# Heads of q and k crossed between the slots of a tile at the load, v loaded as it lies

## The chip, the cores and the metric

The kernel runs on one core of a Trainium2 chip, in one launch. The time is the device time of one execution in microseconds; the median of several executions is compared. The core has five engines with an instruction stream each: TensorE (PE in the profile, its weight loads PEld), VectorE (DVE), ScalarE (ACT), GpSimd (POOL) and SyncE (SP), which here issues DMAs. Sixteen DMA engines move the data. An engine takes its instructions strictly in the order of its stream and waits where one's input is not there yet.

## The reference

Eight batches, eight heads, 576 tokens, 64 numbers per head. First a Nystrom attention with 32 landmarks, each the mean of 18 neighbouring tokens; then a normalization and a two-layer network over the 512 features of all heads, added to the attention's output.

```python
q_lm = q.reshape(B, H, 32, 18, D).mean(axis=3)        # k_lm likewise
A  = softmax(scale * q    @ k_lm.T)                   # 576 x 32
Bm = softmax(scale * q_lm @ k_lm.T)                   # 32 x 32
C  = softmax(scale * q_lm @ k.T)                      # 32 x 576
Z  = Bm.T / (norm_1(Bm) * norm_inf(Bm) + 1e-6)
for _ in range(6): Z = 2 * Z - Z @ Bm @ Z
y  = A @ Z @ C @ v                                    # per head; heads side by side: x
xn = (x - mean(x)) / sqrt(var(x) + 1e-6) * g_ln
out = x + maximum(xn @ w_ch1, 0) @ w_ch2              # w_ch1 512 x 2048, w_ch2 2048 x 512
```

## The kernel before

**Units and tiles.** A unit is four heads of one batch, so a batch has two units (`u` = 0 and 1). Each of q, k and v is loaded per unit as one staging tile `stg` of 128 partitions x 2 slots x 9 x 64 numbers (`load`, L309). The four heads are numbered 2r + e: `e` is the half of the partitions (64 partitions each, nine tokens per partition, which are one row of 2304 bytes in DRAM), `r` the slot in the free dimension. A ring of six staging tiles holds what is on its way; a buffer becomes free when its tile has been cast to fp16. q and k are cast into `nat` tiles by GpSimd, a few by ScalarE, and v into `natv` by GpSimd.

**Attention of batches 1 to 7** is done in sets: batch 1, batch 2, batches 3 and 4, batches 5 and 6, batch 7 (`sets`, class `Coming`). VectorE transposes each `nat` tile in 32x32 blocks into `xT`. After that, TensorE works in tiles of 32x32: partition block p_ of xT holds half of the tokens of one head, and a matmul names its row block `rb` and its column block `cb` in the array; `cb` is also the partition block of PSUM that gets the result. `scores_k` (L965) computes the landmark scores of k (psec), `scores_q` those of q (psea), `attention2` (L1014) the landmark-landmark scores (psb), the product with v (pscv), the iteration for Z (st), and then zt and zc. For units of odd number the column blocks of `scores_k` are turned by two, so that two units work in different places of the array. The transposed scores then hold the two halves of the tokens' partitions exchanged, and for the product with v the odd units' v has to be exchanged likewise: `load_swapped` (L316) loads it in two DMAs of 64 partitions each, L320 (288 KB each).

**zt** (L1130 to L1145): for every unit and head, the transposed product of Z and C v, in one pair of PSUM banks (`pszt`), copied to SBUF in one instruction by the engine that is free sooner (`sooner`). `pszc` is the same product the other way round; masked by `heads_of` it becomes `zcbd`, with which `rows_of` computes the attention's output rows. The first layer of the network never forms the normalized input: `First.products` (L1264) multiplies zt with the scaled w1 per head (`m16`), and `chunk` multiplies `m16` with the scores `ea`.

**The network's layers** run on whole 128x128 arrays: `first_layer` in 16 chunks per batch (psh to hT), `second_layer` over hT and w2. From batch 4 on the second layer uses seven half-size products in place of eight (`seven_products`).

**Order.** The load of batch 0, of the weights and of batch 1 stands in a fixed order in the text (L1723 to L1752): w1, then batch 1's k, k, q, q, three pieces of w2, batch 1's two v tiles, the other five pieces of w2; the casts on GpSimd stand in the same order. Everything after comes from `run()`: five streams (attention, totals, first layers, the first rows, second layers) and helpers (loads, casts, transposes, statistics, stores) are interleaved by a planner while the program is written. It keeps a model of every engine and of the DMA (`Clock`, with bytes at 385 per ns) and takes the next step whose time has come. The table `AFTER` overrules it: an entry (a, i): (b, n) holds step i of stream a back until stream b has taken n steps. What comes out is a fixed instruction order on each engine. Stores and loads share SP's stream.

Of the kernel before, what the change touches and what calls it, by code (L numbers as in the profile page):

```python
# [20 lines left out]
def kernel(  # L21
# [293 lines left out]

    def load_swapped(src, b, u, queue):  # L316
        t = stage.tile([P, 2, NJ, D], FP32, name="stg", tag="stg")
        halves = src[b, 4 * u:4 * u + 4].rearrange("(r e) (t j) d -> e t r j d", e=2, j=NJ)
        for e in range(2):
            keep(queue.dma_start(out=t[ts(1 - e, 64), :, :, :], in_=halves[e]))  # L320
        return t
# [48 lines left out]
    for x in range(2):  # L370
        for e in range(2):
            nc.gpsimd.tensor_copy(out=heads4[:, x, :, e], in_=mask4[:, ts(e ^ x, 2)])
    heads_of = [heads4[:, x, :, :].rearrange("p r e -> p (r e)") for x in range(2)]
    spread16 = const.tile([P, 2, 2, 2, LM], FP16, name="spread16")
    nc.gpsimd.memset(spread16[:], 0.0)
# [397 lines left out]
    class Coming:  # L773
# [91 lines left out]
        def load(self, i, queue=nc.sync):  # L865
            nm, w = self.parts[i]
            b, u = self.units[w]
            src = {"q": q, "k": k, "v": v}[nm]
            self.stg[i] = stage.pin(load_swapped(src, b, u, queue) if nm == "v" and u % 2
                                    else load(src, b, u, queue))  # L870

# [93 lines left out]
    def scores_k(pair, lm, xT):  # L965
        tiles = {w: ps2.tile([P, 2, 512], FP32, name="psec", tag="p2") for w in pair}
        for r in range(2):
            for x in range(2):
                for w in pair:
                    for p_ in range(4):  # L970
                        rows = ts(p_, 32)
                        cb = 32 * ((p_ + 2 * (w % 2)) % 4)
                        MM(tiles[w][ds(cb, 32), r, 0:NJ * LM], lm["q", w][rows, r, :, x],
                           xT["k", w][rows, r, :, :, x], rb=32 * p_, cb=cb,
                           start=(x == 0), stop=(x == 1), skip=True)
# [16 lines left out]
    def scores_q(pair, lm, xT):  # L992
        tiles = {w: ps2.tile([P, 2, 512], FP32, name="psea", tag="p2") for w in pair}
        for s_ in range(2):
            for x in range(2):
                for w in pair:
                    for p_ in range(4):
                        e, half = divmod(p_, 2)
                        r = half ^ s_
                        rows = ts(p_, 32)  # L1000
                        cb = 32 * (2 * (e ^ (w % 2)) + r)
                        MM(tiles[w][ds(cb, 32), half, 0:NJ * LM], lm["k", w][rows, r, :, x],
# [11 lines left out]
    def attention2(bs, c):  # L1014
# [10 lines left out]
        for y in range(W // 2):  # L1025
# [5 lines left out]
            for w in pair:  # L1031
                for x in range(2):
                    for p_ in range(4):
                        rows, r = ts(p_, 32), p_ % 2
                        MM(psb[rows, w, :], lm["q", w][rows, r, :, x], lm["k", w][rows, r, :, x],
                           rb=32 * p_, cb=32 * p_, start=(x == 0), stop=(x == 1), skip=True)
            if y == W // 2 - 1:
# [91 lines left out]
        cv, z0 = cv_[0], 2 * (bs[0] % 2) if W == 2 else 0  # L1129
        yield lambda: clock.both(clock.at(st, cv), asm.next("zt"))  # L1130
        pszt = ps2.tile([P, 2, 512], FP32, name="pszt", tag="p2")

        def cv_of(w, p_, at, n):
            return cv[ts(p_, 32), w, ds((D + 1) * (p_ % 2) + at, n)]

        for w in range(W):
            for p_ in range(4):
                e, r = divmod(p_, 2)
                sl = ds(32 * p_, 32)
                for half in range(2):  # L1140
                    cb = 64 * e + 32 * half
                    MM(pszt[ds(cb, 32), r, ds(LM * w, LM)], cv_of(w, p_, 32 * half, 32), st[sl, w, LM:],
                       rb=32 * p_, cb=cb)
        zt = asm.pin(asm.tile([P, 2, W, LM], FP16, name="zt", tag="zt"))
        sooner(2 * W * LM)(zt[:].rearrange("p r w l -> p r (w l)"), pszt[:, :, 0:W * LM])  # L1145
        pszc = ps2.tile([P, 2, 512], FP32, name="pszc", tag="p2")
        for w in range(W):
            for p_ in range(4):
                sl = ds(32 * p_, 32)
                cb = 32 * ((p_ + 2 * (w % 2)) % 4)  # L1150
                MM(pszc[ds(cb, 32), w % 2, ds(D * (w // 2), D)], st[sl, w, LM:], cv_of(w, p_, 0, D),
# [9 lines left out]
        for w in range(W):  # L1161
            dve.tensor_tensor(
                out=zcbd_buf[z0 + w][:],
                in0=pszc[:, w % 2, None, ds(D * (w // 2), D)].broadcast_to([P, 4, D]),
                in1=heads_of[w % 2][:, :, None].broadcast_to([P, 4, D]),
                op=ALU.mult)
# [78 lines left out]
    class First:  # L1245
# [18 lines left out]
        def products(self, f, psm):  # L1264
# [3 lines left out]
            for r in range(2):  # L1268
                for e in range(2):
                    for u, (w, _) in enumerate(self.units):  # L1270
                        rows, cb = ds(64 * e, 64), 32 * (2 * (e ^ u) + r)
                        MM(psm[u][ds(cb, 32), :], self.zt[rows, r, w, :],
# [301 lines left out]
    def help_out(hurry=False):  # L1574
# [68 lines left out]
    AFTER = {  # L1643
        (0, 21): (4, 68), (0, 64): (4, 197), (0, 66): (2, 79), (0, 72): (4, 251),
        (0, 80): (4, 269), (0, 93): (4, 314), (0, 101): (4, 496), (0, 108): (4, 528),
        (0, 116): (2, 149), (2, 25): (0, 3), (2, 28): (4, 16), (2, 66): (4, 129),
        (2, 89): (4, 219), (2, 96): (0, 82), (2, 108): (4, 333), (3, 5): (4, 2), (4, 10): (0, 13),
        (4, 33): (0, 16), (4, 140): (0, 40), (4, 171): (0, 55), (4, 433): (2, 133),
        (5, 19): (0, 31), (5, 24): (2, 53), (9, 8): (4, 238),
    }  # L1650
# [134 lines left out]
```

## Time and profile before

| | |
|---|---|
| median of three runs | 272.34 us (270.92 to 272.78) |
| profiled execution | 272.2 us |
| its span, first to last instruction | 270.5 us |
| TensorE busy | 257.0 us, 95% |
| VectorE, ScalarE, GpSimd busy | 202.9, 174.0, 133.9 us |
| DMA packets of the SP queue | 23288, 46.02 MB, 55.5% of sixteen engines' span |
| DMAs issued | 146 |

The profile is one execution. The row PE of its slices shows TensorE's busy share in 40 slices of 6.76 us, in tenths; the row DMA the mean busy share of the sixteen DMA engines; GB/s what they moved. A completion of a DMA is itself a small packet and is counted with the packets under 512 B. "Idle before" in a timeline, in brackets behind an instruction, is the time for which its engine had nothing to do, and what ended it. Lines L296 and L302 are helpers through which all instructions of the engines pass, so the tiles' names tell the groups apart.

### The profile page before, as it was taken

The page shows a single profiled execution, that of the slowest core. Times are in us where ns is not written, and L with a number is a line of the kernel's source. Part 1 is how long each engine was busy: PE and PEld are TensorE (multiplying, and loading weights), DVE is VectorE, ACT ScalarE, POOL GpSimd, SP SyncE. Part 2 cuts the span into 40 slices and gives each one's busy share as a digit, 9 for nine tenths or more (in the row PEclk, how much of TensorE's full clock was granted, in tenths as well). Part 3 has the DMA queues.
Part 4 walks back from the last instruction along what each step waited for, and adds up shares of the span by engine and source line. Part 5 has one row for each costly group of instructions (what it writes and reads, how often), then busy time and mean ns, then how long its engine had stood idle before and what let it go on. Part 6 is the DMA issues. An engine that isn't in the chain of part 4 may idle for free.

```text
span 270.5 us, 8330 instructions
## 1 busy us (share of the span) xinstructions
PE 257.0 (95%) x3442; PEld 167.7 (62%) x3442; DVE 202.9 (75%) x461; ACT 174.0 (64%) x335; POOL 133.9 (49%) x161
## 2 busy tenths in 40 slices
PE   6789996999999999999999999999999999999992
PEld 6644663456553674546655456687868865788881
DVE  2557772599999996998973896799863699948751
ACT  2578893377856978589987659678488645872000
POOL 5286757999947669979999937100000014000000
PEclk9999998899999999999999999999999999999999
DMA  7999999999998998936900120110060006100616
GB/s 252 379 395 376 344 255 385 367 278 311 334 286 224 323 334 246 279 136 197 233 21 22 46 63 16 41 39 4 2 155 0 4 20 148 35 0 17 141 30 166
DMA packets 23486, 46.68 MB, mean 173 GB/s; under 512 B 2324, under 2 KB 2584, under 8 KB 23448
## 3 DMA queue, kind: packets, MB, share of 16 engines
q1 hardware_dynamic: 23288, 46.02, 55.5%
q8 instruction: 27, 0.44, 0.7%
q10 hardware_dynamic: 160, 0.13, 0.2%
q14 instruction: 11, 0.09, 0.1%
HBM read 36.70 MB, written 9.44 MB: 171 GB/s over the span
## 4 chain that ended last, share of the span: by engine, by line
PE 56%; DVE 18%; DMA 12%; ACT 5%; issue 3%; POOL 2%; SPq 1%; ACTq 0%; POOLq 0%; DVEq 0%
PE bank L302 37%; PE psh L302 14%; DMA stg<-in_v_dram 6%; DMA stg<-in_q_dram 3%; DMA wstg<-in_moe_w_ch_dram 3%; DVE m L296 3%; DVE part L296 3%; DVE xblk L296 2%; DVE xT L296 2%; ACT hT L296 2%; DVE six L296 2%; PE psd L302 1%; ACT xblk L296 1%; PE pscv L302 1%; DVE hT L296 1%
## 5 line engine op out<-in xcount | busy, mean ns | idle before, releaser
L302 PE MATMUL bank<-w,hT 128*128 128x512 f16 (+3 forms) x528 | 111.1, 335 | 2.5 <-POOL w L296 2.5
L296 ACT ACTIVATE hT<-psh 128x576 f16<-128x576 f32 x115 | 71.5, 654 | 19.0 <-PE psh L302 17.9
L302 PEld LDWEIGHTS <-hT 128*128 128x128 f16 x656 | 60.4, 98 | 34.4 <-issue 9.7
L302 PE MATMUL psh<-ea,m 128*128 128x288 f16 x512 | 78.6, 286 | 0.9 <-DVE ea L296 0.5
L302 PEld LDWEIGHTS <-m 128*128 128x128 f16 x512 | 48.9, 97 | 20.4 <-issue 3.9
L296 DVE SCALAR_TENSOR_TENSOR xblk<-bank,rstd,xblk 128x256 f32<-128x256 f32 (+2 forms) x77 | 39.2, 541 | 20.4 <-PE bank L302 17.6
L296 POOL TENSOR_TENSOR ea<-ea,lns 128x576 f16<-128x576 f16 x14 | 18.2, 1309 | 56.0 <-ACT lns L296 53.7
L296 POOL CAST nat<-stg 128x1152 f16<-128x1152 f32 x23 | 26.5, 1164 | 7.9 <-DVE sT L296 5.0
L296 DVE BATCH_NORM_STATS2 six<-xblk 128x6 f32<-128x512 f32 x36 | 24.2, 673 | 2.6 <-ACT xblk L296 2.6
L296 POOL CAST natv<-stg 128x1152 f16<-128x1152 f32 x16 | 18.2, 1163 | 13.2 <-DMA stg<-in_v_dram 10.5
L296 ACT COPY xblk<-bank 128x512 f32<-128x512 f32 (+1 forms) x35 | 20.0, 595 | 4.6 <-PE bank L302 4.2
L296 DVE STREAM_TRANSPOSE xT<-nat 128x576 uint32<-128x576 uint32 x28 | 21.2, 757 | 0.0
L302 PE MATMUL bank<-w2mix 128*128 128x256 f16 x128 | 17.4, 273 | 0.0
L296 ACT ACTIVATE lns<-psd 128x576 f32<-128x576 f32 x16 | 10.3, 646 | 9.4 <-PE psd L302 9.3
L296 DVE SCALAR_TENSOR_TENSOR st<-st,bank 128x128 f16<-128x128 f16 (+2 forms) x36 | 11.0, 307 | 6.5 <-PE bank L302 6.2
L302 PE MATMUL bank<-w2mix,hT 128*128 128x256 f16 x128 | 15.8, 273 | 0.0
L296 ACT ACTIVATE ea<-psea 128x576 f16<-128x576 f32 x14 | 8.4, 650 | 10.3 <-PE psea L302 10.3
L296 ACT CAST m<-bank 128x512 f16<-128x512 f32 x19 | 10.4, 587 | 6.6 <-PE bank L302 6.5
L302 PE MATMUL bank<-zcbd,ea 128*128 128x256 f16 x80 | 14.5, 273 | 0.0
L296 DVE TENSOR_REDUCE part<-xT 128x32 f16<-128x576 f16 x20 | 14.3, 744 | 0.2
L296 DVE SCALAR_TENSOR_TENSOR m<-less,zsum,bank 128x512 f16<-128x512 f16 (+1 forms) x18 | 11.5, 678 | 3.5 <-ACT hT L296 1.4
L302 PEld LDWEIGHTS <-w2mix 128*128 128x128 f16 x128 | 12.4, 98 | 2.1 <-issue 0.2
(135 smaller groups left out, 361.9 us busy)
## 6 DMA issues: line engine op xcount, KB each, us to landing
stg<-in_q_dram SPq DMA_DIRECT2D x16, 576.0 KB, 6.4
stg<-in_k_dram SPq DMA_DIRECT2D x16, 576.0 KB, 6.7
out_dram<-xblk SPq DMA_DIRECT2D x70, 128.0 KB, 2.4
wstg<-in_moe_w_ch_dram SPq DMA_DIRECT2D x16, 512.0 KB, 8.4
stg<-in_v_dram SPq DMA_DIRECT2D x9, 576.0 KB, 8.3
stg<-in_v_dram SPq DMA_DIRECT2D x14, 288.0 KB, 7.8
out_dram<-xblk ACTq DMA_DIRECT2D x1, 96.0 KB, 2.4
out_dram<-xblk SPq DMA_DIRECT2D x1, 96.0 KB, 2.3
```

What stands on the lines that cost most here:

```text
L296: return lambda *args, **kw: keep(getattr(self.engine, op)(*args, **kw))
L302: keep(nc.tensor.matmul(o, l, r, start=start, stop=stop, tile_position=(rb, cb), skip_group_check=(skip or cb != 0)))
```

## The change

- `load_crossed` replaces `load` for q and k of batches 1 to 7. Slot r of unit u takes heads 0 and 3 of the unit where r = u, and heads 1 and 2 where not, one DMA per slot over all 128 partitions. Batch 0 still uses `load`.
- v is loaded with `load` everywhere; `load_swapped` is gone.
- The column blocks of the scores of k, of q, of psb, of pszc and of the products of heads follow the new places of the heads. In `scores_k` the loop over x is outside that over r.
- zt's matmuls go to four PSUM banks (two of the pair, two of the single banks) and are copied in three instructions; the step waits for two free banks as well.
- A small mask `crossed4` is built at the start, by eight GpSimd copies, and replaces `heads_of` for batches 1 to 7.
- `AFTER` has 30 entries in place of 24; one of them is the same.

```diff
-    def load_swapped(src, b, u, queue):
+    def load_crossed(src, b, u, queue):
         t = stage.tile([P, 2, NJ, D], FP32, name="stg", tag="stg")
-        halves = src[b, 4 * u:4 * u + 4].rearrange("(r e) (t j) d -> e t r j d", e=2, j=NJ)
-        for e in range(2):
-            keep(queue.dma_start(out=t[ts(1 - e, 64), :, :, :], in_=halves[e]))
+        for r in range(2):
+            o = r ^ u
+            heads = src[b, 4 * u + o:4 * u + 4 - o:3 - 2 * o]
+            keep(queue.dma_start(out=t[:, r, :, :].rearrange("p j d -> p (j d)"),
+                                 in_=heads.rearrange("e (t j) d -> e t (j d)", j=NJ)))
         return t
...
-            self.stg[i] = stage.pin(load_swapped(src, b, u, queue) if nm == "v" and u % 2
-                                    else load(src, b, u, queue))
+            self.stg[i] = stage.pin((load if nm == "v" else load_crossed)(src, b, u, queue))
...
-        for r in range(2):
-            for x in range(2):
+        for x in range(2):
+            for r in range(2):
...
-                        cb = 32 * ((p_ + 2 * (w % 2)) % 4)
+                        cb = 32 * (p_ ^ 2 * (w % 2 ^ r))
...
-                        cb = 32 * (2 * (e ^ (w % 2)) + r)
+                        cb = 32 * (2 * (e ^ (w % 2)) + (r ^ e))
...
-        yield lambda: clock.both(clock.at(st, cv), asm.next("zt"))
-        pszt = ps2.tile([P, 2, 512], FP32, name="pszt", tag="p2")
+        yield lambda: clock.both(clock.at(st, cv), asm.next("zt"), banks.next(2))
+        n = W // 2 * LM
+        t = ps2.tile([P, 2, 512], FP32, name="pszt", tag="p2")
+        pszt = [[t[:, e, 0:n] for e in range(2)], [banks.take([P, n]) for _ in range(2)]]
...
-                    cb = 64 * e + 32 * half
-                    MM(pszt[ds(cb, 32), r, ds(LM * w, LM)], cv_of(w, p_, 32 * half, 32), st[sl, w, LM:],
+                    cb = 64 * (e ^ r ^ w % 2) + 32 * half
+                    MM(pszt[w % 2][e][ds(cb, 32), ds(LM * (w // 2), LM)], cv_of(w, p_, 32 * half, 32), st[sl, w, LM:],
                        rb=32 * p_, cb=cb)
...
-        sooner(2 * W * LM)(zt[:].rearrange("p r w l -> p r (w l)"), pszt[:, :, 0:W * LM])
+        zt_ = zt[:].rearrange("p e (y x) l -> p e y x l", x=2)
+        for e in range(2):
+            sooner(n)(zt_[:, e, :, 1, :], pszt[1][e].rearrange("p (y l) -> p y l", l=LM))
+        sooner(2 * n)(zt_[:, :, :, 0, :], t[:, :, 0:n].rearrange("p e (y l) -> p e y l", l=LM))
...
-                        rows, cb = ds(64 * e, 64), 32 * (2 * (e ^ u) + r)
+                        rows = ds(64 * e, 64)
+                        cb = 32 * (2 * (r ^ u) + (e ^ u) if self.b else 2 * (e ^ u) + r)
...
-        (0, 21): (4, 68), (0, 64): (4, 197), (0, 66): (2, 79), (0, 72): (4, 251),
-        (0, 80): (4, 269), (0, 93): (4, 314), (0, 101): (4, 496), (0, 108): (4, 528),
...
+        (0, 64): (4, 199), (0, 72): (4, 250), (0, 80): (4, 268), (0, 100): (4, 503),
+        (2, 25): (4, 7), (2, 66): (4, 129), (2, 93): (4, 229), (2, 96): (0, 77),
...
```

## The prediction

> **What bounds it now.** I read the page's slices first, then TensorE's waits with the timeline around its largest, then the DMA rows, and last the stretches with their transfer rates.
>
> ```profile
> PE   6789996999999999999999999999999999999992
> DMA  7999999999998998936900120110060006100616
> GB/s 252 379 395 376 344 255 385 367 278 311 334 286 224 323 334 246 279 136 197 233 21 22 46 63 16 41 39 4 2 155 0 4 20 148 35 0 17 141 30 166
> DMA packets 23486, 46.68 MB, mean 173 GB/s; under 512 B 2324, under 2 KB 2584, under 8 KB 23448
> ...
> stg<-in_v_dram SPq DMA_DIRECT2D x9, 576.0 KB, 8.3
> stg<-in_v_dram SPq DMA_DIRECT2D x14, 288.0 KB, 7.8
> ...
> g_rows<-in_moe_g_ln_dram SPq DMA_DIRECT2D x1, 2.0 KB
> ```
>
> TensorE is full from 44 us on, except where the last output drains. The DMA engines are full for the first 100 us: in that time the kernel has as much to load as it can load. TensorE's only large hole, in slice 7, is a load's:
>
> ```profile
> 39.14 1.17 POOL L296 CAST natv<-stg 128x1152 f16<-128x1152 f32 x1 [2.00 <-DMA stg<-in_v_dram]
> 41.68 1.16 POOL L296 CAST natv<-stg 128x1152 f16<-128x1152 f32 x1 [1.38 <-DMA stg<-in_v_dram]
> 42.79 1.04 POOL L296 CAST w<-wstg 128x1024 f16<-128x1024 f32 x1
> ...
> 43.88 0.59 PE L302 MATMUL bank<-w,hT 128*128 128x512 f16 x2 [2.55 <-POOL w L296]
> ```
>
> TensorE waits for a cast of w2 on GpSimd, which is queued behind the cast of batch 1's second v tile; that one waited for its DMA. These v tiles are loaded as two halves of 64 partitions:
>
> ```profile
> core 0: us, PE busy (x) PEld busy (x) DVE busy (x) ACT busy (x) POOL busy (x), PEclk, DMA share, GB/s
> ...
> 34.00:40.00 6.00, 6.00 (x99) 3.60 (x96) 4.42 (x16) 5.82 (x16) 2.99 (x4) 1.00 1.05 249
> 44.00:50.00 6.00, 6.00 (x115) 2.71 (x113) 1.75 (x7) 3.28 (x6) 4.86 (x5) 0.72 1.06 391
> ```
>
> Both stretches have all sixteen engines busy (share 1.05 and 1.06), but while the halves travel they move 249 GB/s instead of 391. So how a transfer's rows are laid out decides its rate, whatever its bytes.
>
> **The loads: what gets better.** Each odd v tile becomes one DMA over 128 partitions. In the 6 us of the row above, 6 x (391 - 249) = 0.85 MB were lost, 2.2 us at 391 GB/s. Batch 1's natv cast would come at 39.5 instead of 41.68, the w2 cast 2.2 us earlier, and the hole of 2.55 us would shrink to about 0.4 us. The other six odd v tiles gain as much DMA time and no TensorE time: from 60 to 244 us TensorE is busy 183.47 of 184 us.
>
> **The loads: what gets worse.** Each of the 28 q and k tiles of batches 1 to 7 now comes in two DMAs, one per slot: 28 more for q and k, 7 fewer for v, 167 instead of 146. At 0.37 to 0.6 us each the 21 cost SP about 10 us, hidden under the 111 us that SP waits for VectorE's finished blocks. The cost lies in the shape. One of the two DMAs takes heads 4u+1 and 4u+2, neighbours in DRAM: 128 rows of 2304 B in one row of equal steps, as in the old load. The other takes heads 4u and 4u+3, a step of three heads: on the DRAM side its outermost dimension counts 2, and under it come 64 rows. The old loads, stores and weights all count 128 or 64 outermost. Only one DMA counts fewer: g_rows, four rows. The page shows what that does. The issues listed in its DMA part add up to 146, and every completion is a packet of under 512 B; 2324 of them are 145 x 16 + 4. So 145 DMAs finished on sixteen engines and the four-row one on four: an engine gets whole outer rows. By this row the pieces with an outermost 2 run on two engines.
>
> The Trainium skill says so outright ("DMA: Bandwidth & Descriptors", section "Why a DMA increments its semaphore by 16 and not by 1"): the number of engines is the largest up to 16 that divides the slowest dimension of both sides, and they are the lowest-numbered. By that rule the pieces run on two engines and the sum is the one below; the trace agrees as far as the 2324 goes, and no run here yet shows a DMA with a short dimension on one side alone.
>
> Price of a piece: 391 GB/s over sixteen is 24.4 GB/s an engine; 294,912 B on two take 6.04 us, on sixteen 0.75 us. A q or k tile then holds the two engines 6.8 us instead of 1.5. Bounds: nothing added (all sixteen) and, with the engine rate of the 249 GB/s row (15.6), 9.5 us a piece; I take 6.04, the rate of full-width transfers, since the pieces write 128 partitions.
>
> The account of these two engines, which work their transfers off in order: batch 1's first k tile begins at about 25 us (its cast waited for it until 27.20). Up to batch 6's last q: 24 tiles x 6.8 = 163; v of batches 1 to 4, 8 x 1.5 = 12; w2, 8 x 1.34 = 11; 14 stores of 0.34 = 5. It lands at 25 + 163 + 12 + 11 + 5 = 216 us. With a cast (1.15 us) its transpose can start at 217. Before, that transpose (the 24th of the 28 of xT) stood here in VectorE's order:
>
> ```profile
> 135.12 0.77 DVE L296 STREAM_TRANSPOSE xT<-nat 128x576 uint32<-128x576 uint32 x1
> ```
>
> The order on every engine is fixed when the program is written, and the planner's clock knows bytes, not engines, so VectorE stands there until 217: 82 us late. Queued behind it are the relu, residual and statistics steps of earlier batches, so TensorE stops too; its buffers let it run a few us ahead (I take 4, from bounds 0 and 15, nearer the small end since it has two PSUM pairs). What follows is TensorE's: busy 130 of the 135.4 us left, with nothing to win back. Batch 7's tiles land by 216 + 4 x 6.8 + 4 x 1.5 = 249, about when a transpose at 163.4 + 82 asks for them: 0 to 5 more, cover for which is that TensorE needs them only at 212 + 82. So 272.2 - 4 + 82 = **350 us**, in the profiled execution's time (272.2, span 270.5 and 1.7 around it; the median 272.34 is the same within 0.1%).
>
> **The rest** is small. zt is copied in three pieces instead of one: for two units 3 x 0.215 against 0.265 to 0.291 us, for four 2 x 0.215 + 0.265 against 0.362; over five sets 1.8 us more on ScalarE or VectorE, of which TensorE can see at most the second and third copy (bounds 0 and 1.8; TensorE waited for zt 1.2 us in all, I take 0.5). The wait for two free banks is part of the planner's order, and behind it stands the set's own chain, at a point where second-layer products can go first. The zt, psb, pszc and q-score products only change places in the array: sixteen of pszt last 0.23 us where one lasts 0.17, eight products of heads 0.41 where one lasts 0.39, so they overlap fully already; bounds plus or minus 0.05 us a group, value 0. Of k's scores the first slot ends two groups later, 0.1 to 0.2 us, in seven pairs. Eight tiny GpSimd copies at the start (0.18 us each by the heads row) lie in its 6.85 us of idleness before v arrives; uncovered they would cost 1.4. The order table moves steps among TensorE's own work: bounds -3 to +5 us (nothing is left to win after 44 us but 0.5; a wrong step can cost a hole like the 2.55), value 0.
>
> **Rivals.**
> *All sixteen engines serve the crossed pieces.* Then only the first part counts: 272.2 - 2.2 + 0.5 = 270.5, 267 to 277 with the order table's bounds. For it: every DMA of 64 or 128 rows here has sixteen completions, and the destination still counts 128. Against it: the four-row one. This is the side where it is not slower, and it turns on one number, completions per crossed piece.
> *Both pieces run on two engines*, if the neighbours' 128 rows are also given as 2 x 64: a tile takes 12.1 us, batch 6's last q lands at 25 + 290 + 28 = 343, 208 us late: 476. Against it: the natural load has the same neighbours and counts 128.
> *The new order puts a step too early*: sixteen engines, but a hole or two of 2.5 us: 275 to 277.
>
> **Numbers.** Two engines for one piece of each tile 0.64; both pieces 0.07; sixteen 0.29, split into faster by over 1% 0.12, within 1% 0.11 and slower 0.06 (the order). One per cent is about what a measurement of this kernel can tell from no change (270.92 to 272.78 without any). So faster 0.12, same 0.11, slower 0.77. The likeliest case's own range is 330 to 385: below, faster packets (25.5 GB/s an engine at best, -7) and TensorE further ahead (-11); above, batch 7's loads, the clock after holes (0.72 in the stretch after the 2.55 us one) and DMA engines left idle by SP's stores. To leave out no more than 2 in 10 the range must also take in the sixteen-engine case: 267 to 385.
>
> **What would show it.** Right: DMA completions, as the count under 512 B: 28 x 2 + 138 x 16 + 4 = 2268; at sixteen 166 x 16 + 4 = 2660, with both pieces short 1876. GB/s under 100 from 25 us on, with a DMA share near 0.2; k and q issues landing after 20 us or more; GpSimd's nat casts waiting for DMA; TensorE at a few tenths between 30 and 215, then full. Wrong: 2660 completions, TensorE full from 42 us, and its hole before the w2 product gone (first part right) or still 2.5 us (that part wrong too). A time over 400 would mean both pieces; one of 300 to 325 that the order after lets TensorE work far ahead of the stuck loads.

## The result, and the profile after

The changed kernel takes 388.79 us (388.12 to 389.26), against 272.56 (270.92 to 274.33) before in the same comparison: a ratio of 1.426 [1.417, 1.436]. The prediction was 350 with a range that ended at 385. The mechanism it forecast is there in the count of completions and in GpSimd's waits for loads; the size is 39 us short.

The page of after: TensorE's busy tenths in 40 slices of 9.67 us, its granted clock, the DMA engines' share, what they moved, and the count of packets.

```profile
PE   8873649983700549999440059399999999999995
...
PEclk9997669997665558999765559799999999999999
DMA  8953777145333139423335544511211040410045
GB/s 302 384 209 101 203 221 257 60 147 157 97 126 102 51 109 286 141 74 107 104 101 160 183 139 128 177 53 42 45 29 30 1 110 3 98 41 2 16 94 137
DMA packets 23430, 46.68 MB, mean 121 GB/s; under 512 B 2268, under 2 KB 2528, under 8 KB 23392
```

The last line decides the main question: 2268 packets under 512 B is 28 x 2 + 138 x 16 + 4, so each of the 28 pieces with heads 0 and 3 finished on two engines. The bytes are the same 46.68 MB. The load that filled the first 100 us of before now stretches over 250 us, and so long TensorE stands still again and again (slices 3 to 26), at a clock of 0.5 to 0.7 around its holes; its busy time grows from 257.0 to 279.8 us.

The same rows of a narrower stretch, 150 to 200 us of after, in 40 slices of 1.25 us:

```profile
DMA  9992512896111111115911116411159211111111
GB/s 295 326 318 97 148 57 66 248 253 232 48 52 52 52 58 52 50 52 160 332 57 63 52 50 168 117 65 50 51 136 352 68 63 52 52 50 50 52 50 52
```

Here one sees the two engines by themselves. In 24 of the 40 slices the share is one tenth (two of sixteen would be 0.125), and the rate there is mostly 50 to 52 GB/s; in between, the neighbours' piece goes over all sixteen. At 52 GB/s the piece of 294,912 B takes 5.7 us.

After's waits, the engine that waited, for what, and us in total, times, longest:

```profile
POOL nat L296 <- DMA stg<-in_k_dram: 48.9, 10, 6.9
POOL nat L296 <- DMA stg<-in_q_dram: 47.0, 9, 7.3
...
PE pszt L302 <- ACT lns L296: 26.6, 1, 26.6
```

GpSimd's casts of q and k wait 95.9 us for their loads, 5 us a time. TensorE's longest wait, though, names ScalarE and not a load. That one leads to the 39 us (below).

### The profile page after: what moved, and what is told of

Its sections match the earlier page's. It is cut to its first block, busy times and chain, and to the rows that moved or that the text cites. A ratio compares the mean times of both kernels' runs of the same rounds, so it can differ in the third digit from the quotient of the medians.

```text
span 386.7 us, 8370 instructions
## 1 busy us (share of the span) xinstructions
PE 279.8 (72%) x3441; PEld 176.8 (46%) x3441; DVE 203.0 (53%) x461; ACT 177.0 (46%) x344; POOL 137.6 (36%) x170
## 2 busy tenths in 40 slices
DMA packets 23430, 46.68 MB, mean 121 GB/s; under 512 B 2268, under 2 KB 2528, under 8 KB 23392
## 4 chain that ended last, share of the span: by engine, by line
DMA 46%; PE 27%; SPq 10%; POOL 9%; DVE 3%; issue 2%; ACT 2%; POOLq 0%; ACTq 0%
DMA stg<-in_q_dram 21%; DMA stg<-in_k_dram 19%; PE bank L302 18%; SPq L321 8%; PE psh L302 7%; POOL w2mix L296 4%; DMA stg<-in_v_dram 4%; POOL asum L296 2%; DMA wstg<-in_moe_w_ch_dram 2%; POOL nat L296 1%; SPq L311 1%; ACT hT L296 1%; PE pscv L302 1%; DMA out_dram<-xblk 1%; POOL w L296 1%
## 5 line engine op out<-in xcount | busy, mean ns | idle before, releaser
L302 PE MATMUL bank<-w,hT 128*128 128x512 f16 (+3 forms) x528 | 120.9, 354 | 0.0
L302 PE MATMUL psh<-ea,m 128*128 128x288 f16 x512 | 86.5, 302 | 14.3 <-ACT hT L296 6.8
L302 PEld LDWEIGHTS <-hT 128*128 128x128 f16 x656 | 62.3, 101 | 34.2 <-issue 12.1
L302 PEld LDWEIGHTS <-m 128*128 128x128 f16 x512 | 51.5, 103 | 39.8 <-issue 13.0
L296 ACT ACTIVATE lns<-psd 128x576 f32<-128x576 f32 x16 | 10.3, 646 | 47.6 <-POOL ea L296 37.4
L296 ACT COPY xblk<-bank 128x512 f32<-128x512 f32 (+1 forms) x38 | 21.7, 597 | 10.6 <-DMA out_dram<-xblk 6.7
L302 PE MATMUL bank<-nat,pairs 128*128 128x128 f16 x72 | 7.9, 281 | 23.8 <-POOL nat L296 16.8
L302 PE MATMUL pszt<-st,cv 32*32 32x32 f16 x72 | 1.4, 189 | 26.6 <-ACT lns L296 26.6
L296 ACT CAST nat<-stg 128x1152 f16<-128x1152 f32 x4 | 4.6, 1148 | 32.8 <-DMA stg<-in_q_dram 23.6
L302 PEld LDWEIGHTS <-pairs 128*128 128x128 f16 x72 | 6.8, 128 | 26.5 <-issue 25.7
L302 PEld LDWEIGHTS <-zeros 128*128 128x128 f16 x52 | 5.6, 124 | 24.6 <-issue 22.6
L296 DVE TENSOR_TENSOR zcbd<-pszc,crossed 128x256 f16<-128x256 f32 x14 | 5.1, 417 | 21.4 <-PE pszc L302 21.4
```

Of the source, the lines that this page charges most:

```text
L296: return lambda *args, **kw: keep(getattr(self.engine, op)(*args, **kw))
L302: keep(nc.tensor.matmul(o, l, r, start=start, stop=stop, tile_position=(rb, cb), skip_group_check=(skip or cb != 0)))
```

## The experiments

Each diff shows the lines that matter. Not shown are lines that only keep the planner's clock as it was, so that the order on the engines stays.

**Only the pieces with heads 0 and 3.** In after, both slots take neighbouring heads; heads are then paired with another head's v, and everything else of the change stays, the order on every engine too.

```diff
-            heads = src[b, 4 * u + o:4 * u + 4 - o:3 - 2 * o]
+            heads = src[b, 4 * u + 2 * r:4 * u + 2 * r + 2]
```

> The changed kernel, but both slots of a q or k tile take neighbouring heads (2r and 2r + 1), so each of the two DMAs reads 128 rows at equal steps. The number of DMAs, their bytes and the order on all five engines stay; the heads in the tile no longer fit the places that the scores give them, so another function is computed. Theory (a DMA with an outermost dimension of 2 runs on two engines): short packets 166 x 16 + 4 = 2660, every q and k tile about 1.5 us on the wire, time 268 to 275, likeliest 270.5 (the v halves' 2.2 us gained, 0.5 lost on zt). Rival (two DMAs of 288 KB per tile, or the new order, or zt and the new column blocks make the kernel slow): 380 to 390, with 2268 or 2660.

Measured: 268.19 us, ratio to before 0.986 [0.983, 0.988]. This is the lower end of what was expected, with one packet more than the 2660. Its page, TensorE and the packets:

```profile
PE   7889999999999999999999999999999999999993
...
DMA packets 23823, 46.68 MB, mean 175 GB/s; under 512 B 2661, under 2 KB 2921, under 8 KB 23785
```

The timeline of its GpSimd, the casts of batch 1's v and of w2 (start, duration, in brackets the idle time before):

```profile
35.93 1.17 POOL L296 CAST natv<-stg 128x1152 f16<-128x1152 f32 x1 [0.44 <-DMA stg<-in_v_dram]
37.43 1.17 POOL L296 CAST natv<-stg 128x1152 f16<-128x1152 f32 x1 [0.34 <-DMA stg<-in_v_dram]
38.79 1.04 POOL L296 CAST w<-wstg 128x1024 f16<-128x1024 f32 x1 [0.19 <-DMA wstg<-in_moe_w_ch_dram]
```

The second v cast comes at 37.43 instead of 41.68, the w2 cast at 38.79 instead of 42.79, and the hole of 2.55 us is gone. So the whole slowdown is the step of three heads on the DRAM side; zt in four banks, the new column blocks, `crossed4` and the order table together cost nothing that shows. Without the step the change would gain 1.4%, but it is the step that makes it compute the right thing.

**The same step in the kernel before.** Before, with its own order, and only the load of q and k crossed.

```diff
-            self.stg[i] = stage.pin(load_swapped(src, b, u, queue) if nm == "v" and u % 2
-                                    else load(src, b, u, queue))
+            self.stg[i] = stage.pin(load_swapped(src, b, u, queue) if nm == "v" and u % 2
+                                    else load(src, b, u, queue) if nm == "v"
+                                    else load_crossed(src, b, u, queue))
```

> The kernel before, with q and k of batches 1 to 7 loaded crossed as in the change and nothing else changed: old order, old zt, old column blocks, v still in halves. The heads do not fit their places, so another function is computed. Theory (the load alone does it): 380 to 395, with 28 x 2 + 145 x 16 + 4 = 2380 short packets. Rival (the new order or zt has a share): clearly under 380, by as much as that share.

Measured: 396.27 us (one run), 1 us above what was expected; 2380 packets under 512 B, as expected. The crossed load alone makes more than the whole slowdown, whichever order stands behind it.

**The outermost dimension as a dose.** In after, the slow piece is read as other rows of the same size: 32 rows of four heads, or 16 rows of eight heads; and once both pieces as two rows.

```diff
-            heads = src[b, 4 * u + o:4 * u + 4 - o:3 - 2 * o]      # pieces with o == 0
+            rows = src[b, 4 * u:4 * u + 4].rearrange("e (t j) d -> e t (j d)", j=NJ)[:, 0:32, :]
or
+            rows = src[b, 0:8].rearrange("e (t j) d -> e t (j d)", j=NJ)[:, 0:16, :]
or, for both pieces
+            heads = src[b, 4 * u + r:4 * u + r + 3:2]
```

> The changed kernel, but the DMA that took heads 0 and 3 takes sixteen rows of each of the eight heads of the batch: outermost 8 on the DRAM side, same bytes, same order, other data in q and k. Theory: eight engines, 28 x 8 + 138 x 16 + 4 = 2436 short packets; a piece takes 1.5 us, a tile 2.3 instead of 6.8; batch 1's four tiles cost 3 us more than in the kernel before, its v 2.2 less: 271 to 278, likeliest 273. Rival (it is the jump between distant heads in DRAM that is slow): as slow as the changed kernel or slower, 388 and over, since it jumps seven times per DMA instead of once.

> The same with 32 rows of each of the unit's four heads: outermost 4. Theory: four engines, 28 x 4 + 138 x 16 + 4 = 2324 short packets; a piece 3.0 us, a tile 3.8. By the account of those engines batch 6's last q lands at 25 + 24 x 3.8 + 28 = 144; GpSimd can then begin the normalization of ea of batches 3 and 4 at about 151 instead of 116: 34 us late, 300 to 312, likeliest 306. Rival (distance in DRAM): 388 and over.

> The changed kernel, but both slots take heads two apart (0 and 2, 1 and 3): both DMAs of a tile have an outermost 2. Other data in q and k. Theory: 56 x 2 + 110 x 16 + 4 = 1876 short packets, a tile holds the two engines 12.1 us, batch 6's last q lands at 25 + 290 + 28 = 343, the normalization of ea of batches 3 and 4 at 350 instead of 116: 234 us late, 490 to 520, likeliest 506. Rival (the stretch of 117 us comes from the order or from other parts, and loads only add to it): 388 plus at most some tens.

| outermost dimension of the pieces | packets under 512 B | time, us | above 268.2 | added piece time in 24 tiles, us |
|---|---|---|---|---|
| 128 and 128 | 2661 | 268.19 | | |
| 8 and 128 | 2436 | 285.38 | 17 | 18 |
| 4 and 128 | 2324 | 316.31 | 48 | 54 |
| 2 and 128 (after) | 2268 | 388.79 | 121 | 127 |
| 2 and 2 (one run) | 1876 | 529.1 | 261 | 254 |

The packet counts are those of 8, 4 and 2 engines, to the packet. The last column is the prediction's arithmetic for batches 1 to 6 (an engine at 24.4 GB/s): 0.75, 2.27, 5.29 and 10.58 us a tile more than sixteen engines need. Nearly all of it reaches the end. The expectation for eight rows, 271 to 278, took only batch 1's tiles to count and the other loads to have room; from the table they have next to none. The rival, distance in DRAM, is refuted: eight rows jump seven times per DMA and are the fastest of the short ones. Four rows came out 4 us above what was expected, both pieces short 9 us above. By the Trainium skill, the number of engines is the largest up to sixteen that divides the slowest dimension on both sides ("DMA: Bandwidth & Descriptors", section "Why a DMA increments its semaphore by 16 and not by 1"). Counts and times of these runs agree at 2, 4 and 8, with 128 rows on the other side in each.

**Can the step be kept without the two engines?** After, its function kept, with the piece loaded as two DMAs of one head on 64 partitions each.

```diff
...  # only for pieces with o == 0
+            for e in range(2):
+                queue.dma_start(out=t[ts(e, 64), r, :, :].rearrange("p j d -> p (j d)"),
+                                in_=src[b, 4 * u + 3 * e].rearrange("(t j) d -> t (j d)", j=NJ))
```

> The changed kernel, its function and its order kept, but the piece with heads 0 and 3 is loaded in two DMAs of one head, 64 rows to 64 partitions each. Theory: sixteen engines each, 194 x 16 + 4 = 3108 short packets. These pieces write half of the partitions, as v's halves did before: at 249 instead of 391 GB/s they cost 0.43 us more a tile, 1.7 us over batch 1's four tiles, against 2.2 us gained at v: 269 to 275, likeliest 271.5. Rival: what is left of the change (order, zt, two and three DMAs per tile on SP) costs more than the v halves: 275 to 280.

Measured: 278.74 us, 1.024 [1.018, 1.029]: slower than before, and the rival's number, but not for the rival's reason, since the order and zt cost nothing that shows with neighbouring heads. Its page, the DMA engines:

```profile
DMA  7999999999999799984801111110051060100616
GB/s 262 374 395 290 259 380 354 250 284 278 294 248 365 233 281 286 372 256 122 271 3 41 42 41 41 41 39 2 0 127 31 4 144 11 41 0 2 153 39 155
```

All sixteen engines are busy, at 250 to 290 GB/s in many slices: the half-partition loads, which the change took away from v, come back with q and k. The expectation had counted their price of 0.43 us a tile in batch 1 alone; in 24 tiles it is 10.3 us, and 278.74 is 10.6 us more than the 268.19 with neighbours. That agreement is an estimate; what the further DMAs cost SP was not tried by itself.

**What v in one piece is worth.** Before, with each odd v tile loaded whole over 128 partitions (its two half heads then lie exchanged, so its products take another head's v).

```diff
-        for e in range(2):
-            keep(queue.dma_start(out=t[ts(1 - e, 64), :, :, :], in_=halves[e]))
+        queue.dma_start(out=t[:], in_=src[b, 4 * u:4 * u + 4].rearrange("(r e) (t j) d -> (e t) r j d", e=2, j=NJ))
```

> The kernel before, with the odd units' v loaded in one DMA over 128 partitions; its heads then lie exchanged, so another function is computed. Order kept. Theory (the halves cost 2.2 us of transfer time, which TensorE's hole before the w2 product shows): the hole shrinks from 2.55 to about 0.4 us and the time from 272.3 to 270. Rival (the w2 cast waits for its own DMA as well, which the freed wire does not bring sooner): no difference, 272.

Measured: 268.3 us, 0.988 [0.984, 0.992]. From 34 to 40 us it moves 390 GB/s instead of 249. The gain that the change was able to bring is 3 to 4 us.

**Two halves at once.** Before, the second half of batch 1's odd v tile issued from GpSimd, ahead of its casts of the first w2 pieces, so that both halves are under way together.

```diff
-            keep(queue.dma_start(out=t[ts(1 - e, 64), :, :, :], in_=halves[e]))
+            (nc.gpsimd if e and b == 1 else queue).dma_start(out=t[ts(1 - e, 64), :, :, :], in_=halves[e])
```

> The kernel before, its function kept, with one thing changed: the second half of batch 1's odd v tile is issued from GpSimd's queue right behind its cast of batch 1's last q tile, while the first half comes from SP as before, so that both halves of the partitions are written at the same time. Order kept. Theory (two halves under way together use all partitions and travel at about 390 GB/s instead of 249, which brings the w2 cast 2 us forward): the hole of 2.55 us shrinks to 0.5 or less, 268.5 to 270.5. Rival (the two queues share the engines in turns but each packet is as slow as before, or GpSimd's issue costs what is won): 271 to 273.

Measured: 272.45 us, 1.003 [0.999, 1.006]. The stretch from 34 to 40 us (its columns: length, busy us and instructions of each engine, clock, DMA share, GB/s):

```profile
34.00:40.00 6.00, 5.88 (x93) 3.23 (x80) 4.88 (x17) 5.50 (x14) 2.88 (x3) 1.00 1.07 227
```

TensorE's timeline behind it:

```profile
43.29 1.01 PE L302 MATMUL bank<-w,hT 128*128 128x512 f16 x2 [3.41 <-POOL w L296]
```

No gain: 227 GB/s instead of 249, and the hole is 3.4 us instead of 2.55. The same page of the Trainium skill ("Rules for kernel authors") says of two transfers to the two partition halves that they share the same engines and don't help each other; this run agrees.

### Where do the 39 us above 350 come from?

The first four runs started from after's longest hole, 26.6 us before pszt, and took one suspected wait away at a time.

*The products that normalize ea of batches 3 and 4* stand on GpSimd, in its queue behind the casts of batches 5 and 6. They are put on VectorE at the same places in the program:

```diff
-                normalize(ea[w], pool)
+                normalize_on_dve(ea[w]) if bs == (3, 4) else normalize(ea[w], pool)
```

> The changed kernel, but the normalization of ea for batches 3 and 4 (four products) runs on VectorE instead of GpSimd, at the same place in the order; loads as in the change. Theory (TensorE's hole of 26.6 us at 199 comes from GpSimd's order, where those products stand behind the casts that wait for batch 5's and 6's loads): the hole shrinks to 7 us or less, VectorE's last two transposes of that set then bind as I had predicted, 366 to 372. Rival (the transposes in VectorE's order were the limit all along): 385 to 390, the hole stays.

Measured: 388.66 us. The hole of 26.6 us is down to 1.4, and not a microsecond is won: the rival's number, though the hole it spoke of went. The holes that took its place, in TensorE's timeline:

```profile
223.62 0.58 PE L302 MATMUL bank<-zcbd,ea 128*128 128x256 f16 x2 [4.98 <-ACT xblk L296]
234.09 0.59 PE L302 MATMUL bank<-part,spread 128*128 128x256 f16 x2 [9.89 <-ACT xblk L296]
241.74 0.59 PE L302 MATMUL bank<-part,spread 128*128 128x256 f16 x2 [5.97 <-ACT xblk L296]
250.64 1.12 PE L302 MATMUL psh<-ea,m 128*128 128x288 f16 x4 [5.45 <-ACT hT L296]
```

ScalarE's copies before the first two of these:

```profile
222.99 0.59 ACT L296 COPY xblk<-bank 128x512 f32<-128x512 f32 x1 [5.91 <-DMA out_dram<-xblk]
233.46 0.59 ACT L296 COPY xblk<-bank 128x512 f32<-128x512 f32 x1 [9.88 <-DMA out_dram<-xblk]
```

ScalarE waits for a buffer of an output block that a store has not read yet. My reading is that the stores' rows on the two busy engines stand behind pieces of 5.7 us, so that a slow load delays a store, and through it TensorE; without the stores (next) no hole of TensorE there ends on them.

*Without the stores* of the first 27 of 36 blocks (the third expectation below says 32; the kernel writes 36), in after and in the kernel just described, and then with ea of batches 5 and 6 on VectorE too:

```diff
+            if j < 27:
+                continue
-                normalize_on_dve(ea[w]) if bs == (3, 4) else normalize(ea[w], pool)
+                normalize_on_dve(ea[w]) if bs in ((3, 4), (5, 6)) else normalize(ea[w], pool)
```

> The changed kernel without the stores of the first 27 of 36 output blocks (these rows of the output are not written). Loads as in the change, order kept but for the stores. Theory (the two engines also hold up the stores, whose few rows there queue behind batch 7's q and k pieces; ScalarE waits for the block buffers that they free, 6.7 us, and TensorE with it at 243 to 250): that hole goes, the one at 199 to 225 (GpSimd's order) stays: 379 to 384. Rival (stores do not matter, batch 7's loads themselves hold the end up): 386 to 390.

> The same without those stores, and the normalization of ea of batches 3 and 4 on VectorE as well. With the normalization alone moved, the hole at 199 closed from 26.6 to 1.4 us and 26 us of new holes came behind it, each ending when a store landed. Theory (GpSimd's order and the block buffers are two covers over the same limit): with both gone, 358 to 368, where VectorE's wait for batch 6's last transposes (at about 218) is what is left, as the prediction had it. Rival (a third wait takes their place, batch 7's loads): 380 and over.

> The kernel after, without the stores of its first 27 blocks of out, and with the products that normalize ea in batches 3 to 6 (four pairs of tiles) all on VectorE at their places instead of GpSimd. What is left out is 27 of 32 blocks of the output. Theory (the time of the kernel after is set by GpSimd's fixed order: the casts of batch 7's q and k, which land late, stand ahead of the w2mix subtractions, 18 us, and of the ea products of batches 5 and 6): without the stores and without batches 3 and 4's products on GpSimd, TensorE's hole of 21.0 us at 252.7 to 273.7 waited for those products alone, so it closes to a few us and the time falls from 383 by about 15 to 20 us, to 360 to 368. Rival (the DMA account itself, or another wait that stands at the same place, is what decides): 378 to 384, with a hole of over 10 us after 250 that ends on something other than ea of batches 5 and 6.

Measured: 383.37, 382.96 and 377.3 us, one run each. The first is as expected. TensorE's longest hole after 250 us in the second:

```profile
273.72 2.08 PE L302 MATMUL psh<-ea,m 128*128 128x288 f16 x8 [21.03 <-ACT lns L296]
```

The same in the third:

```profile
279.03 0.63 PE L302 MATMUL bank<-w,zt 64*32 64x512 f16 x7 [9.74 <-DVE xblk L296]
```

In the second, GpSimd casts batch 7's last q at 248.72, sums it, works on w2mix until 270.6, and only then comes to ea of batches 5 and 6. In the third, VectorE waits 8.1 us for batch 7's natv cast, which is behind the same w2mix. Each wait that was taken away was followed by another behind the same late tiles; three of them together gave 11.5 us. The theory that one wait stood behind the hole missed its numbers in three of these four runs; the rival of yet another wait was right in the second, and the third lies between both.

So the next runs took the late tiles themselves. **Batch 7 fast, batches 1 to 6 slow, and the other way round:**

```diff
             heads = src[b, 4 * u + o:4 * u + 4 - o:3 - 2 * o]
+            if b == 7:          # in the other run: b < 7
+                heads = src[b, 4 * u + 2 * r:4 * u + 2 * r + 2]
```

> The kernel after with batch 7's four q and k tiles in neighbouring heads (two pieces of 128 equal rows), batches 1 to 6 as they are in after; it computes another function for batch 7, with the same bytes, instructions and order but for two pairs of loads that stand in another order beside SP's stores. It asks where the 39 us between the prediction (350) and the result come from. Prediction's own step (batch 6's last q, cast at 218.3, sets the end and batch 7's tiles are covered): taking batch 7's slow pieces away changes nothing beyond what the prediction left out, so TensorE's end stands at 272.2 - 4 + 82, 345 to 355 only if batch 7 was the whole of the miss. Theory (batch 7's casts on GpSimd, with w2mix and ea of batches 5 and 6 behind them, set the end): the last q cast of batch 7 comes at about 226 instead of 254.7, 93 us later than before instead of 121, and with 4 to 5 us of GpSimd's slack the time is 358 to 364. Rival (every slow piece costs about 0.8 of its added time at the end, wherever it stands): 388.8 - 4 x 5.3 x 0.8 = 372, 369 to 376.

> The complement: after with neighbouring heads in batches 1 to 6, and only batch 7's four q and k tiles with a piece on two engines; it computes another function for batches 1 to 6. Theory (a slow piece costs nothing where the kernel loads ahead of its need): with all neighbours batch 7's pieces were issued at 103 to 121 and its casts came at 122.8 to 129.1, so four pieces of 6.04 us fit almost before their casts; the last cast comes at 130 to 133 and the time is 268 to 273. Rival (0.8 of the added time reaches the end wherever a piece stands): 268.2 + 4 x 5.3 x 0.8 = 285, 281 to 289. Completions under 512 B: 4 x 2 + 162 x 16 + 4 = 2604.

Measured: 378.86 us (377.95 to 379.59) with batch 7 fast; 269.55, or 0.991 [0.987, 0.995] of before, with batch 7 alone slow. Four slow tiles cost 1.4 us where the kernel loads ahead of its need, and 9.9 us where everything is late already: a slow transfer has no price of its own. The first number lies above all three expectations. Batches 1 to 6 alone give 379, so batch 7 is 10 of the 39 us and no more. The hole is the old one, from 199.7 to 226.5. GpSimd's timeline in this kernel, from the cast of batch 6's last q on:

```profile
219.17 1.15 POOL L296 CAST nat<-stg 128x1152 f16<-128x1152 f32 x1 [2.98 <-DMA stg<-in_k_dram]
220.40 1.15 POOL L296 TENSOR_TENSOR asum<-nat 128x512 f32<-128x512 f16 x1
221.63 1.25 POOL L296 TENSOR_TENSOR asum<-asum 128x256 f32<-128x256 f32 x2
222.96 0.42 POOL L296 TENSOR_TENSOR s<-asum,nat 128x128 f16<-128x128 f32 x1
223.32 1.16 POOL L296 CAST natv<-stg 128x1152 f16<-128x1152 f32 x1
224.44 2.52 POOL L296 TENSOR_TENSOR ea<-ea,lns 128x576 f16<-128x576 f16 x2
```

TensorE's instruction that ends the hole:

```profile
226.45 0.23 PE L302 MATMUL pszt<-st,cv 32*32 32x32 f16 x8 [26.73 <-ACT lns L296]
```

Batch 6's last q is cast, summed, one v is cast, and then come the products of ea of batches 3 and 4, whose scores were done long ago. The profile puts the cast's wait down to a load of k; by its place in the order the tile is the last q, for which after names its load:

```profile
218.26 1.15 POOL L296 CAST nat<-stg 128x1152 f16<-128x1152 f32 x1 [2.37 <-DMA stg<-in_q_dram]
```

ScalarE's `lns` waits for a buffer that these products free (36.9 us in after), and TensorE for ScalarE. The same stretch of GpSimd's timeline in the kernel before:

```profile
113.03 1.16 POOL L296 TENSOR_TENSOR asum<-nat 128x512 f32<-128x512 f16 x1
114.27 1.26 POOL L296 TENSOR_TENSOR asum<-asum 128x256 f32<-128x256 f32 x2
115.61 0.43 POOL L296 TENSOR_TENSOR s<-asum,nat 128x128 f16<-128x128 f32 x1
116.40 1.29 POOL L296 TENSOR_TENSOR ea<-ea,lns 128x576 f16<-128x576 f16 x1 [0.37 <-ACT lns L296]
```

The sums of batch 6's last q (ScalarE casts this tile there, at 111.05) began at 113.03 before and begin at 220.40 here, 107.4 later; the whole execution is 107.2 longer. GpSimd's queue has no room at this place. The last two runs take the products of ea off it, with batch 7 fast:

> Batch 7's q and k in neighbouring heads (as before this run, another function for batch 7 only) and the four products that normalize ea of batches 3 and 4 on VectorE instead of GpSimd. With batch 7 fast alone the time was 378.9, and TensorE's hole of 26.7 us ended on ea of batches 3 and 4, which stand in GpSimd's queue behind batch 6's last q: the sums of that tile began at 113.0 before and at 220.4 there, 107 later, as much as the whole slowdown. Theory (what decides is the place of batch 6's last q in GpSimd's queue, which has no room, and not its transpose at 135 in VectorE's, which has 22 us): the hole closes, and the next thing in the same queue is late next: batch 7's casts, w2mix and ea of batches 5 and 6, some 97 to 101 us late, 366 to 373. Rival (batch 6's transpose on VectorE sets the end, as the prediction had it): 345 to 355. Second rival (ea's place doesn't matter, the DMA account does): 377 to 380.

> The same with the products of ea of batches 5 and 6 on VectorE too. Theory (GpSimd's queue): now only w2mix and batch 7's natv casts are left in it behind the late q and k; they end at about 258, TensorE goes on at about 261, and from the like point it needed 97 us in the run with batches 3 to 6 on VectorE and all tiles slow: 356 to 363. Rival (the transposes on VectorE): 345 to 355. Second rival (DMA account): 372 to 380.

Measured: 369.31 and 374.54 us, one run each. With ea of batches 3 and 4 on VectorE the long hole is gone, as the theory has it, and the time is in its range; TensorE has no hole over 0.8 us after 227.5. What is left shortly before, in TensorE's timeline:

```profile
222.49 0.38 PE L302 MATMUL bank<-zcbd,ea 128*128 128x256 f16 x2 [3.15 <-ACT xblk L296]
227.50 0.59 PE L302 MATMUL bank<-part,spread 128*128 128x256 f16 x2 [4.64 <-ACT xblk L296]
```

And in ScalarE's:

```profile
221.85 0.59 ACT L296 COPY xblk<-bank 128x512 f32<-128x512 f32 x1 [3.96 <-DMA out_dram<-xblk]
226.87 0.59 ACT L296 COPY xblk<-bank 128x512 f32<-128x512 f32 x1 [4.43 <-DMA out_dram<-xblk]
```

These are the stores behind batch 6's pieces again (in the run without stores and with the same products on VectorE, TensorE came to the first of these two part,spread products at 215.41 instead of 227.50 and to the second at 220.35 instead of 229.58; 3.2 us of this is the tile's own earlier arrival, since its cast started at 215.48 instead of 218.63). What the second waited for there was the late tile itself, its sums, in `part`:

```profile
220.35 0.61 PE L302 MATMUL bank<-part,spread 128*128 128x256 f16 x2 [4.07 <-DVE part L296]
```

But the theory's next step, that w2mix and ea of batches 5 and 6 would now be what is late, fell: TensorE waits for neither after 227.5, and with the latter off GpSimd too the time was 5.2 us longer, in the second rival's range of 372 to 380. (The two runs of the kernel with four rows differ by over 4 us, so this step is small.) One of these products took 1.83 us on VectorE where GpSimd took 1.3, the others 0.7 to 0.8, and between VectorE's products TensorE has a new hole of 2.1 us at 260.5. Only the hole is shown; where the rest went stays open.

How late the same instruction is, against the kernel with neighbouring heads, whose order they share:

| instruction (start, us) | neighbours | after | batch 7 fast | and ea of 3, 4 on VectorE |
|---|---|---|---|---|
| cast of batch 6's last q, GpSimd | 107.2 | +111.0 | +112.0 | +111.4 |
| zcbd of batches 3 and 4, VectorE | 118.4 | +108.8 | +109.7 | +88.1 |
| cast of batch 7's last q, GpSimd | 129.1 | +125.6 | +110.2 | +105.4 |
| zcbd of batches 5 and 6, VectorE | 167.0 | +120.1 | +111.4 | +101.3 |
| end of the profiled execution | 268.2 | +120.2 | +111.2 | +101.1 |

Lateness is fixed by the time that zcbd of batches 5 and 6 is made, and from there to the end nothing is lost or won back.

## Why the prediction was right and wrong

**Two engines for the piece with heads 0 and 3 (0.64).** Right, shown three ways: 2268 packets as forecast, 52 GB/s at a share of one tenth, and the dose of 8, 4 and 2. The price of a piece, 6.04 us, measures 5.7; a tile, 6.8, measures 7.1 in batches 5 and 6, with the stores between them (eight casts from 168.6 to 218.3 us). The rival of sixteen engines, and the one of holes from the order table, are refuted; the one with both pieces on two engines, 476, can be compared with the run made so: 529.

**The account of the two engines.** "It lands at 25 + 163 + 12 + 11 + 5 = 216 us" and its transpose "can start at 217": the cast of batch 6's last q starts at 218.3. The sum is good to 2 us; its parts were not measured one by one.

**The place on the path failed.** "Before, that transpose (the 24th of the 28 of xT) stood here in VectorE's order": 135.12. But the same tile stands on GpSimd first, and GpSimd, too, has a fixed order with other batches' work behind it. There its sums began at 113.03. The same 217, by which the tile is cast, taken at GpSimd's place, gives 217 - 113 = 104 us late and 272.2 + 104 = 376, against 378.9 measured with batch 7 fast. The transpose had 22 us in hand, and the prediction took the step with the most room in the chain cast, sums, transpose instead of the one with the least.

**The lead of 4 us failed.** "its buffers let it run a few us ahead (I take 4, from bounds 0 and 15 ...)". There is no lead at the end: with batch 7 fast the end is 111.2 us late when the cast is 112.0.

**Batch 7 failed.** Its tiles were to be "0 to 5 more, cover for which is that TensorE needs them only at 212 + 82". They cost 9.9 us in after (388.8 less 378.9). The load's time was right enough (249 forecast, the last cast at 254.7); but GpSimd needs them out of the way earlier than TensorE needs their content: behind their casts stand w2mix and the products of ea of batches 5 and 6, for which TensorE waited 21.03 us in the second run without stores. How the 9.9 us divide between GpSimd and the stores is not shown.

**The sum again, as the runs give it.** With after's order and no slow piece: 268.2. The 24th transpose starts at 219.8 in the run without ea of batches 3 and 4 on GpSimd, and at 127.4 in the kernel with neighbours, 92.4 later: 360.6. That is what the prediction meant to work out, and no run shows it by itself: none leaves out the stores, GpSimd's products and batch 7's slow pieces together. The nearest is the second part,spread product in the run without stores and with the products on VectorE: it comes at 220.35, and at 129.90 with neighbours, 90.5 us later. Of the prediction's miss, 10.6 us are the lead of 4, the transpose that stands 7.7 us earlier in after's order, and 2.8 us of later arrival, less 4.0 by which the first part did better. The two holes behind stores, 3.15 + 4.64: 368.4, measured 369.3. GpSimd's queue, 9.6: 378.9. Batch 7, 9.9: 388.8. The last two steps are differences of measured runs; the ones before are worked out from starts. The waits cover one another: GpSimd's place alone gives 376, but only 9.6 us came off when its products were moved, with the two holes behind stores left to stand.

**The first part, "2.2 us earlier" and a hole of "about 0.4 us".** Right in place, and about half too small: the casts come 4.0 to 4.3 us earlier in the kernel with neighbours, the hole is gone, and the kernel gains 3.8 us (v alone in before: 3.0).

**The rest, about 0.** Right: zt's three copies, the column blocks, `crossed4`, the order table and 21 more DMAs leave 268.2 with neighbours, no more than with v alone (268.3).

**What was to be seen.** "GB/s under 100 from 25 us on, with a DMA share near 0.2" was too simple: between the slow pieces the neighbours' pieces, v and w2 go over all sixteen engines, and the mean of a slice is 51 to 286. "TensorE at a few tenths between 30 and 215, then full": full from 250 on. "k and q issues landing after 20 us or more" can't be read: the page of after gives no landing times.

## What to carry to other kernels

A load's cost is in the shape of both its sides: a slice with a step over two heads in DRAM put a DMA with 128 partitions on two engines, and the count of small packets shows it before any time does. When a tile becomes late, look for its first use in every engine's queue and take the place with the least room; with fixed orders, what stands behind a cast there may belong to quite another batch. And where one wait is covered by the next, taking waits away one by one tells little: make the late thing early for one stage, and compare the same instructions' starts stage by stage.

## What the runs showed of the hardware that was not expected

- ScalarE's copies waited for stores 6.7 us in after and 29.0 us, at most 9.9 at a time, with ea of batches 3 and 4 on VectorE; before and with neighbouring heads, not at all. That the stores stand behind pieces on the two engines is my reading.
- While v's two halves of 64 partitions travelled, all sixteen engines were busy (share 1.05 to 1.07) at 249 GB/s from one queue and 227 from two; in the same stretch loads to 128 partitions moved 388 and 390 (with neighbours, and with v whole in before).
- TensorE's granted clock fell with its holes: mean 0.854 in after and 0.763 with both pieces on two engines, against 0.999 with neighbours. In after it stays at 0.97 to 1.00 once TensorE is full again (250 us on), and its busy time of 131.0 us from there to the end is that of the last 136 us with neighbours, 131.5. So the 23.3 us that it is busy longer in all lie before, among the holes; whether any of the 120 us is the clock's by itself is not shown.
